# Moving the attention projections next to MLP1 in four groups of a fused transformer block

## The chip, the cores and the metric

The kernel runs on one core of a Trainium2 chip. The metric is the device time of one execution in microseconds (us), the median of several executions; the traces are hardware profiles of one execution each.

## The reference, cut to what matters

```python
x = A_x                                            # 1 x 2048 x 576, bfloat16
h = x + attention(layernorm(x), A_wqkv) @ A_wo     # 32 heads of 18, window of 8 keys, 2 apart
y = layernorm(h)                                   # called LN2 below
h2 = h + gelu(y @ B_w1 + B_b1) @ B_w2 + B_b2       # MLP1: 576 -> 4608; MLP2: 4608 -> 576
```

## The kernel before

The 2048 rows are 16 tiles of 128, worked off in eight groups of two. I number the groups from 1; the code's `k` is one less. A group's stretch on TensorE is MLP1 (`pm` in the profile, 64-row tiles), MLP2 (`po`, 128 rows), and somewhere in it the output projection of the attention (`pw`, 64-row tiles) of the *next* group's two tiles, called c and d. VectorE computes the attention of later groups meanwhile, and LN2 of c and d follows the projection: VectorE adds x (`ln2_h`), ScalarE takes the statistics (`ln2_act`), GpSimd the inverse root, ScalarE writes the normalised tile (`ln2_send`), which is stored to memory and read back transposed (`hnT`) as the input of the next group's MLP1.

In groups 3 to 8 MLP2 is a fast matrix product of the Strassen-Winograd kind: for a part of the rows (`rows`: 12 of 18 blocks in groups 4 and 5, 16 in group 6, all in 7 and 8) seven products instead of eight, and the rest as plain products.

```python
    PRODUCTS = {
        1: (lambda m: h_block(0, 0, m, m + 1), lambda m: w2_block(0, 0, m, m + 1)),
        2: (lambda m: h_block(1, 0, m, m + 1), lambda m: w2_block(1, 0, m, m + 1)),
        3: (lambda m: s_slot(3, m, m + 1), lambda m: w2_block(1, 1, m, m + 1)),
        4: (lambda m: h_block(1, 1, m, m + 1), lambda m: t_slot(3, m, m + 1)),
        5: (lambda m: s_slot(0, m, m + 1), lambda m: t_slot(0, m, m + 1)),
        6: (lambda m: s_slot(1, m, m + 1), lambda m: t_slot(1, m, m + 1)),
        7: (lambda m: s_slot(2, m, m + 1), lambda m: t_slot(2, m, m + 1)),
    }
    # ...
    def product(n, bank, m0, m1):
        lhs, rhs = PRODUCTS[n]
        for m in range(m0, m1):
            mm(bank, lhs(m), rhs(m), n in (1, 7) and m == 0, m == m1 - 1)

    def plain(i, half, bank, rows):
        for m in range(rows, NM):
            for odd in range(2):
                mm(bank, h_block(odd, i, m, m + 1), w2_block(odd, half, m, m + 1), False, m == NM - 1 and odd == 1)
```

The products share PSUM banks. Products 1 and 2 both add to bank `a`; a ScalarE copy "b" carries what product 1 alone made into bank `b`, on which product 6 goes on; "d" carries that to product 5's bank.

```python
    def mlp2_fast(g, rows, tags, wo, hooks):
        p, q, r, s = tags
        last = wo is None
        j0, j1 = g
        af = psum_pair(q, "po")
        a, f = (af[:, n, 0:HALF] for n in range(2))
        b, d = psum_pair(p, "po")[:, 0, 0:HALF], None
        o0, o1 = (late.tile([P, D], BF16, tag="o_sb", name="o_sb", bufs=2) for _ in range(2))
        bank = {1: a, 2: a, 3: f, 4: b, 6: b}
        # ... (sums into the outputs cut)
        def take():
            bank[7], bank[5] = (psum_pair(tag, "po")[:, 0, 0:HALF] for tag in (r, s))

        lo, hi, all_ = (0, SR), (SR, rows), (0, rows)
        seed = {"b": (1, 6), "d": (6, 5), "f": (5, 3)}
        does = {
            "wo": lambda: wo((r, s)), "e": take, "rest": do_rest, "o1": out1,
            "o0": lambda: out0(int(last), 2), "lo": lambda: out0(0, 1),
            "11": lambda: plain(0, 0, a, rows), "12": lambda: plain(0, 1, f, rows),
            "21": lambda: plain(1, 0, b, rows), "22": lambda: plain(1, 1, bank[5], rows),
        }
        if SR < rows < NM:
            steps = [(1, all_), "b", "wo", "h", "e", (2, all_), "11", (6, lo), (7, lo), "6", "7", (6, hi), "d", (7, hi), "rest", "in",
                     (5, all_), "f", "exp", (4, all_), "21", "22", "o1", "4", (3, all_), "12", "o0", "3"]
        elif rows <= SR:
            steps = [(1, all_), "b", "wo", "h", "e", (2, all_), "11", (6, all_), "d", "6", "7", (7, all_), "rest", "in",
                     (5, all_), "f", "exp", (4, all_), "21", "22", "o1", "4", (3, all_), "12", "o0", "3"]
        elif not last:
            steps = [(1, lo), "wo", (1, hi), "b", "h", "e", (7, lo), (6, all_), "d", "6", "7", (2, all_), (7, hi), "rest", "in",
                     (5, all_), "f", (4, all_), "o1", (3, all_), "o0"]
        else:
            steps = ["e", (1, lo), (7, lo), (1, hi), "b", "h", (7, hi), "rest", (6, all_), "d", (2, all_), "lo",
                     (5, all_), "f", (4, all_), "o1", (3, all_), "o0"]
        for step in steps:
            if isinstance(step, tuple):
                product(step[0], bank[step[0]], *step[1])
            elif step in seed:
                nc.scalar.copy(out=bank[seed[step][1]], in_=bank[seed[step][0]])
            else:
                call([does[step]] if step in does else hooks.get(step, ()))
```

`"wo"` is the projection, `"h"`, `"6"`, `"7"`, `"in"` are places for other engines' work, `"e"` takes the two PSUM pairs that the projection wrote. There are four PSUM pairs in all. What stands at those places, cut:

```python
            rows = ROWS[k]
            home = k % 2
            x = {n: [] for n in ("h", "6", "7", "in", "exp", "4", "3")}
            if k < 6:
                if k == 3:
                    m1[0] += [c_(w2_sums, 8, 12)]
                m1[0] += [c_(pv_sum, d), c_(send_o, d), c_(read_o, d)]
                m1[1] = [c_(accumulate_hs, *g)] if k == 2 else []
                m1[1] += [c_(att_qk_one, f, 1, home ^ 1), c_(att_max, (e, f))]
                m1[3] = []
                if k == 2:
                    m1[3] += [c_(w2_sums, 0, 8)]
                early = {2: (), 3: (0,)}.get(k, (0, 2))
                m1[3] += [c_(h_sums, 0, min(rows, SR), early)]
                x["h"] += [c_(h_sums, 0, min(rows, SR), [t for t in range(4) if t not in early])]
                if k == 5:
                    m1[1] += [c_(w2_sums, 12, 14)]
                    x["h"] += [c_(h_sums, SR, rows), c_(w2_sums, 14, 16)]
                x["exp"] += [c_(exps, e, f), c_(att_den, e, f)]
                # ... (attention of later groups, group 7 and 8's sums cut)
            wo = None
            if c is not None:
                if k == 6:
                    x["h"] = [c_(ln2_h, c), c_(ln2_act, c), c_(ln2_h, d)] + x["h"] \
                        + [c_(ln2_more, d), c_(ln2_rstd, d), c_(ln2_send, c), c_(add_b2, c), c_(add_b2, d), c_(ln2_bias, d)]
                    x["6"] += [c_(ln2_hn, d), c_(ln2_out, d)]
                else:
                    x["h"] = [c_(ln2_stats, c, d)] + x["h"]
                    x["6"] += [c_(ln2_send, c)]
                    x["7"] = [c_(ln2_send, d)] + x["7"]
                x["in"] = [c_(ln2_ins, c, d)] + x["in"]
                wo = lambda tags: wo_visit((c, tags[0]), (d, tags[1]))
            mlp1(g, mlp1_plan(p, q, r, s, (r, s, p)), m1, mid)
            mlp2_fast(g, rows, (p, q, r, s), wo, x)
            p, q, r, s = r, s, p, q
```

Everything is scheduled by hand: each engine runs its instructions in the order of this program.

## Time and profile before

| kernel before | |
|---|---|
| median, three runs | 365.71 us (365.44, 365.71, and 375.73) |
| median, all six runs of the comparison | 365.43 us |
| span of the profiled execution | 363.3 us |
| TensorE busy | 98% |

The unit in which I read this kernel is the stretch from the end of one MLP1 to the end of the next, as TensorE runs in every stretch the same matmuls. In the following view of stretches, one line each for groups 4 to 7, the second number is the length, and then come each engine's busy times.

```profile
199.06:235.55 36.49, 36.49 (x496) 30.11 (x492) 34.58 (x40) 24.03 (x59) 4.47 (x4) 1.00 0.38 87
235.55:272.04 36.49, 36.49 (x496) 30.11 (x492) 33.26 (x39) 24.00 (x59) 3.85 (x4) 1.00 0.36 82
272.04:308.48 36.44, 36.15 (x492) 29.72 (x488) 29.05 (x40) 23.88 (x59) 3.21 (x4) 1.00 0.31 67
308.48:344.23 35.75, 35.75 (x490) 29.53 (x486) 12.41 (x26) 18.43 (x49) 1.43 (x2) 1.00 0.11 29
```

The third busy time is VectorE's.

### The profile page before, as it was taken

What the parts mean: (1) busy time and instruction counts of PE and PEld (TensorE: products, weight loads), DVE (VectorE), ACT (ScalarE), POOL (GpSimd) and SP (SyncE); (2) the same over time, 40 slices, a digit from 0 to 9 for tenths busy, and PEclk for the clock granted to TensorE, in tenths of its full rate; (3) what the DMA queues carried; (4) which work ended last, traced back from release to release, by engine and by line L of the source; (5) the groups of instructions that cost most, each with busy time, mean ns of one, the idle gap of its engine ahead of it and who ended that gap; (6) DMA issues with size and microseconds to landing.
All of it is one profiled execution on the core that took longest, in us unless ns stands there. A gap on an engine that the chain in (4) does not pass through costs nothing.

```text
span 363.3 us, 11427 instructions
## 1 busy us (share of the span) xinstructions
PE 357.6 (98%) x4895; PEld 290.5 (80%) x4895; DVE 300.6 (83%) x426; ACT 228.9 (63%) x507; POOL 39.4 (11%) x47
## 2 busy tenths in 40 slices
PE   8999999999999999999999999999999999999996
PEld 4688877888788877887788778877887788778874
DVE  5999999999999999999999899979998498720431
ACT  4779856799526763668556855685568656615630
POOL 2251004000120030103100211020101010100000
PEclk9999999999999999999999999999999999999999
DMA  7989899964445733720552145304530352030001
GB/s 235 299 204 306 223 260 236 363 219 78 145 89 107 218 111 87 152 40 34 137 106 71 35 125 115 72 32 109 118 71 33 74 102 56 3 89 19 2 2 33
DMA packets 61908, 43.70 MB, mean 120 GB/s; under 512 B 31889, under 2 KB 60177, under 8 KB 61857
## 3 DMA queue, kind: packets, MB, share of 16 engines
q1 hardware_dynamic: 59968, 41.13, 41.1%
q0 software_dynamic: 1728, 1.77, 4.8%
q8 instruction: 38, 0.62, 0.7%
q10 hardware_dynamic: 160, 0.07, 0.1%
q14 instruction: 14, 0.11, 0.1%
HBM read 21.10 MB, written 12.42 MB: 92 GB/s over the span
## 4 chain that ended last, share of the span: by engine, by line
PE 94%; DMA 2%; ACT 1%; SPq 1%; DVE 0%; issue 0%
PE pm L217 39%; PE po L667 25%; PE pq L217 14%; PE po L579 10%; PE pw L217 5%; DMA wq_sb<-in_A_wqkv_dram 1%; SPq L104 1%; PE xt_pt L182 1%; DMA x_all<-b_bc 1%; ACT hn L175 0%; ACT hn L479 0%; PE h_pt L182 0%; PE o_pt L182 0%; DVE h L461 0%; ACT hn L478 0%
## 5 line engine op out<-in xcount | busy, mean ns | idle before, releaser
L560 ACT ACTIVATE h_all<-pm,b_sb 128x256 f16<-128x256 f32 (+1 forms) x288 | 108.3, 496 | 74.3 <-PE pm L217 74.3
L217 PE MATMUL pm<-hnT,w_sb 64*128 64x256 bf16 x2304 | 143.0, 269 | 0.0
L217 PEld LDWEIGHTS <-w_sb 64*128 64x128 bf16 x2304 | 111.6, 94 | 15.1 <-issue 1.7
L667 PEld LDWEIGHTS <-h_all 128*128 128x128 f16 x528 | 50.8, 98 | 14.9 <-issue 2.5
L217 PE MATMUL pq<-wq_sb,xnT 64*128 64x288 bf16 x768 | 54.5, 283 | 0.8 <-DMA wq_sb<-in_A_wqkv_dram 0.7
L217 PEld LDWEIGHTS <-xnT 64*128 64x128 bf16 x864 | 42.4, 94 | 11.3 <-issue 1.1
L351 DVE TENSOR_TENSOR prod<-prod 128x2304 bf16<-128x2304 bf16 (+1 forms) x64 | 44.2, 691 | 2.1
L667 PE MATMUL po<-w2a_sb,h_all 128*128 128x288 bf16 (+1 forms) x302 | 42.0, 286 | 0.0
L397 DVE TENSOR_TENSOR prod<-kv_ring,probs 128x4608 bf16<-128x4608 bf16 x16 | 40.9, 2554 | 0.8 <-DMA kv_ring<-kv_dram 0.5
L345 DVE TENSOR_TENSOR prod<-kv_ring,q_all 128x4608 bf16<-128x4608 bf16 x16 | 40.8, 2549 | 0.2
L217 PE MATMUL pm<-hnT,w1h_sb 64*128 64x256 bf16 x288 | 39.2, 269 | 0.0
L403 DVE TENSOR_TENSOR prod<-prod 128x2304 bf16<-128x2304 bf16 (+1 forms) x32 | 33.8, 1057 | 1.0
L579 PEld LDWEIGHTS <-h_all 128*128 128x128 bf16 x288 | 27.8, 98 | 7.9 <-issue 1.0
L481 POOL TENSOR_TENSOR ln_rstd<-ln_var,mhalf 128x1 f32<-128x1 f32 x13 | 14.5, 1115 | 175.1 <-ACT ln_var L480 175.1
L667 PEld LDWEIGHTS <-kv_ring 128*128 128x128 f16 x240 | 23.5, 98 | 6.4 <-issue 0.5
L579 PE MATMUL po<-w2a_sb,h_all 128*128 128x288 bf16 x224 | 28.5, 286 | 0.0
L647 DVE TENSOR_TENSOR kv_ring<-h_all 128x1536 f16<-128x1536 f16 (+3 forms) x10 | 6.9, 687 | 17.3 <-ACT h_all L560 17.3
L667 PE MATMUL po<-w2b_sb,h_all 128*128 128x288 bf16 (+1 forms) x142 | 21.2, 286 | 0.0
L217 PE MATMUL pw<-wo_sb,oT 64*128 64x288 bf16 x256 | 19.5, 283 | 0.0
L162 POOL TENSOR_TENSOR ln_rstd<-ln_veps,mhalf 128x1 f32<-128x1 f32 (+2 forms) x14 | 13.3, 954 | 48.2 <-DVE ln_veps L156 31.8
L217 PEld LDWEIGHTS <-oT 64*128 64x128 bf16 x288 | 13.5, 94 | 4.8 <-issue 1.7
L739 ACT COPY po<-po 128x288 f32<-128x288 f32 x18 | 6.9, 384 | 16.2 <-PE po L667 13.0
(117 smaller groups left out, 383.1 us busy)
## 6 DMA issues: line engine op xcount, KB each, us to landing
w_sb<-in_B_w_dram SPq DMA_DIRECT2D x6, 768.0 KB, 5.5
kv_ring<-kv_dram SPq DMA_DIRECT2D x28, 144.0 KB, 2.6
w2a_sb<-in_B_w_dram SPq DMA_DIRECT2D x4, 1008.0 KB, 6.6
kv_dram<-kv_ring SPq DMA_DIRECT2D x13, 288.0 KB, 3.3
out_dram<-o_sb SPq DMA_DIRECT2D x15, 144.0 KB, 2.5
td<-q_all SPq DMA_DIRECT2D x14, 144.0 KB, 2.2
td<-hn SPq DMA_DIRECT2D x14, 144.0 KB, 1.8
x_all<-in_A_x_dram SPq DMA_DIRECT2D x12, 144.0 KB, 2.9
```

Of the source, the lines that this page charges most:

```text
L162: nc.gpsimd.tensor_tensor(out=rstd[:], in0=veps[:], in1=mhalf[:].to_broadcast([P, n]), op=ALU.pow)
L217: last = nc.tensor.matmul(duo["g"][r ^ swap][i], lhsT=lhsT, rhs=rhs, start=(swap == 0 and i == 0 and kt == 0), stop=(swap == 1 and kt == K ...
L345: nc.vector.tensor_tensor(out=prod[:], in0=k_ring[j % 2], in1=q_all[:, j, :].unsqueeze(1) .to_broadcast([P, W, D]), op=ALU.mult)
L351: nc.vector.tensor_tensor(out=prod[:, :, o * H:o * H + n], in0=prod[:, :, a * H:a * H + n], in1=prod[:, :, c * H:c * H + n], op=ALU.add)
L397: nc.vector.tensor_tensor(out=prod[:].rearrange("p w (d h) -> p w d h", h=H), in0=v_ring[j % 2].rearrange("p w (d h) -> p w d h", h=H), in ...
L403: nc.vector.tensor_tensor(out=prod[:, 0:n, :], in0=prod[:, 0:n, :], in1=prod[:, n:2 * n, :], op=ALU.add)
L481: nc.gpsimd.tensor_tensor(out=rstd[:], in0=var[:], in1=mhalf[:], op=ALU.pow)
L560: pace[0] = nc.scalar.activation(out=hT(grp)[:, f, 0:N], in_=ps[:, r, i * N:(i + 1) * N], func=ACT.Gelu_apprx_tanh, bias=b1_sb[:, f:f + 1] ...
L579: nc.tensor.matmul(banks[half], lhsT=hT(grp)[:, f, i * P:(i + 1) * P], rhs=w2_rows(f)[:, half * HALF:(half + 1) * HALF], start=(f == 0), s ...
L647: nc.vector.tensor_tensor(out=s_slot(t, m0, m1), in0=a, in1=b, op=alu)
L667: nc.tensor.matmul(bank, lhsT=l, rhs=r, start=start, stop=stop, skip_group_check=True)
L739: nc.scalar.copy(out=bank[seed[step][1]], in_=bank[seed[step][0]])
```

## The change

The intent: every change between 64-row and 128-row work costs TensorE a pause, and a projection in the middle of MLP2 costs two of them more than one that stands right behind MLP1, which works on 64 rows too. Groups 4 to 7 put the projection there. As its time no longer lies between product 1 and product 2, product 7 is put there, and the plain rows go between products 6 and 5. Group 3, the QKV part and the last group keep their orders. The core of the diff (cut: names, the tags' order in the callers, and group 7's own places, where the LN2 statistics are split in the same way and VectorE makes the sums of rows 12 to 18 in four instructions instead of eight):

```diff
-        if SR < rows < NM:
-            steps = [(1, all_), "b", "wo", "h", "e", (2, all_), "11", (6, lo), (7, lo), "6", "7", (6, hi), "d", (7, hi), "rest", "in",
-                     (5, all_), "f", "exp", ...
-        elif rows <= SR:
-            steps = [(1, all_), "b", "wo", "h", "e", (2, all_), "11", (6, all_), "d", "6", "7", (7, all_), "rest", "in",
-                     (5, all_), "f", "exp", ...
+        if rows < NM:
+            steps = [(1, all_), "b", "wo", "hc", "h", "e", (2, all_), "11", (6, all_), "d", "6", "7", (7, all_), "rest"] if rows < SR \
+                else ["wo", "hc", (1, all_), "b", "h", "e", (7, lo), (2, all_), (6, all_), "6", "d", "rest", "7", "11"] if rows == SR \
+                else ["wo", (1, all_), "b", "hc", "h", "e", (7, lo), (2, all_), (6, all_), "6", "d", "7", "11", (7, hi), "rest"]
+            steps += ["in", (5, all_), "f", "exp", ...
         elif not last:
-            steps = [(1, lo), "wo", (1, hi), "b", "h", "e", (7, lo), (6, all_), "d", "6", "7", (2, all_), (7, hi), "rest", "in", ...
+            steps = ["wo", "hc", (1, all_), "b", "h", "e", (7, lo), (6, all_), "6", "d", "7", (2, all_), (7, hi), "rest", "in", ...
 ...
-                early = {2: (), 3: (0,)}.get(k, (0, 2))
+                early = () if k == 2 else (0, 2)
 ...
-                    x["h"] = [c_(ln2_stats, c, d)] + x["h"]
+                    x["hc"] = [c_(ln2_h, c), c_(ln2_act, c)] + x["hc"]
+                    x["h"] = [c_(ln2_h, d), c_(ln2_act, d), c_(put_b2, c), c_(put_b2, d)] + x["h"]
                     x["6"] += [c_(ln2_send, c)]
                     x["7"] = [c_(ln2_send, d)] + x["7"]
```

More of the change, by code (lines that the diff above doesn't have):

```diff
@@ L685, in mlp2_fast @@
     def mlp2_fast(g, rows, tags, wo, hooks):
-        p, q, r, s = tags
         last = wo is None
+        q, p, r, s = tags
         j0, j1 = g
@@ L722, in mlp2_fast @@
         }
-        if SR < rows < NM:
-            steps = [(1, all_), "b", "wo", "h", "e", (2, all_), "11", (6, lo), (7, lo), "6", "7", (6, hi), "d", (7, hi), "rest", "in",
-                     (5, all_), "f", "exp", (4, all_), "21", "22", "o1", "4", (3, all_), "12", "o0", "3"]
-        elif rows <= SR:
-            steps = [(1, all_), "b", "wo", "h", "e", (2, all_), "11", (6, all_), "d", "6", "7", (7, all_), "rest", "in",
-                     (5, all_), "f", "exp", (4, all_), "21", "22", "o1", "4", (3, all_), "12", "o0", "3"]
+        if rows < NM:
+            steps = [(1, all_), "b", "wo", "hc", "h", "e", (2, all_), "11", (6, all_), "d", "6", "7", (7, all_), "rest"] if rows < SR \
+                else ["wo", "hc", (1, all_), "b", "h", "e", (7, lo), (2, all_), (6, all_), "6", "d", "rest", "7", "11"] if rows == SR \
+                else ["wo", (1, all_), "b", "hc", "h", "e", (7, lo), (2, all_), (6, all_), "6", "d", "7", "11", (7, hi), "rest"]
+            steps += ["in", (5, all_), "f", "exp", (4, all_), "21", "22", "o1", "4", (3, all_), "12", "o0", "3"]
         elif not last:
-            steps = [(1, lo), "wo", (1, hi), "b", "h", "e", (7, lo), (6, all_), "d", "6", "7", (2, all_), (7, hi), "rest", "in",
+            steps = ["wo", "hc", (1, all_), "b", "h", "e", (7, lo), (6, all_), "6", "d", "7", (2, all_), (7, hi), "rest", "in",
                      (5, all_), "f", (4, all_), "o1", (3, all_), "o0"]
@@ L1015 @@
             home = k % 2
-            x = {n: [] for n in ("h", "6", "7", "in", "exp", "4", "3")}
+            x = {n: [] for n in ("hc", "h", "6", "7", "in", "exp", "4", "3")}
             if k < 6:
@@ L1040 @@
                 m1[3] = [c_(h_sums, 0, SR)]
-                mid[3] = {1: [c_(h_sums, SR, 16)]}
-                x["h"] += [c_(h_sums, 16, NM)]
+                if k == 7:
+                    mid[3] = {1: [c_(h_sums, SR, 16)]}
+                    x["h"] += [c_(h_sums, 16, NM)]
             if k + 3 < len(GROUPS):
@@ L1048 @@
                 if k == 6:
-                    x["h"] = [c_(ln2_h, c), c_(ln2_act, c), c_(ln2_h, d)] + x["h"] \
-                        + [c_(ln2_more, d), c_(ln2_rstd, d), c_(ln2_send, c), c_(add_b2, c), c_(add_b2, d), c_(ln2_bias, d)]
+                    x["hc"] += [c_(ln2_h, c), c_(ln2_act, c)]
+                    x["h"] += [c_(ln2_h, d), c_(ln2_more, d), c_(ln2_rstd, d), c_(h_sums, SR, NM), c_(ln2_send, c),
+                               c_(ln2_bias, d), c_(add_b2, c), c_(add_b2, d)]
                     x["6"] += [c_(ln2_hn, d), c_(ln2_out, d)]
                 else:
-                    x["h"] = [c_(ln2_stats, c, d)] + x["h"]
+                    x["hc"] = [c_(ln2_h, c), c_(ln2_act, c)] + x["hc"]
+                    x["h"] = [c_(ln2_h, d), c_(ln2_act, d), c_(put_b2, c), c_(put_b2, d)] + x["h"]
                     x["6"] += [c_(ln2_send, c)]
@@ L1058 @@
             mlp1(g, mlp1_plan(p, q, r, s, (r, s, p)), m1, mid)
-            mlp2_fast(g, rows, (p, q, r, s), wo, x)
-            p, q, r, s = r, s, p, q
+            if wo and rows >= SR:
+                mlp2_fast(g, rows, (s, p, q, r), wo, x)
+                p, q, r, s = q, r, p, s
+            else:
+                mlp2_fast(g, rows, (q, p, r, s), wo, x)
+                p, q, r, s = r, s, p, q
 _INS = ['A_x', 'A_wqkv', 'A_wo', 'B_x', 'B_w1', 'B_b1', 'B_w2', 'B_b2']
```

## The prediction

> **What bounds the kernel now.** I number the eight groups of two row tiles from 1, as the title of the change does, so the code's k is one less. I read four views, in this order: the page, the chain that ended last, TensorE's waits, and the timelines of the seams in groups 4 to 7. The page first:
>
> ```profile
> PE 357.6 (98%) x4895; PEld 290.5 (80%) x4895; DVE 300.6 (83%) x426; ACT 228.9 (63%) x507; POOL 39.4 (11%) x47
> PE   8999999999999999999999999999999999999996
> PE 94%; DMA 2%; ACT 1%; SPq 1%; DVE 0%; issue 0%
> ```
>
> TensorE is busy for 98% of the span and is 94% of the chain. The kernel is bound by the stream of matmuls, and the change removes no matmul: the counts per engine of the built programs are equal on TensorE and ScalarE, and VectorE has four instructions fewer. So only time *between* matmuls can be won or lost. The waits of TensorE after the start-up are one line:
>
> ```profile
> PE po L667 <- ACT po L739: 0.3, 1, 0.3
> ```
>
> The columns are the total in us, the number of waits and the longest. One wait for one ScalarE copy. The chain of group 5 (code k = 4), beside that of group 2, where the projection already stands next to MLP1:
>
> ```profile
> 124.51 2.21 PE pw L217 x36
> ...
> 217.92 17.79 PE pm L217 x324
> 235.71 1.58 PE po L667 x12
> 237.29 2.31 PE pw L217 x36
> ```
>
> The columns are start, length, work. The same 36 projection matmuls (pw) take 2.21 us behind MLP1 (pm) and 2.31 us behind a product (po). The timeline of the seam in group 5, TensorE's rows:
>
> ```profile
> 235.65 1.65 PE L667 MATMUL po<-w2a_sb,h_all 128*128 128x288 bf16 x12
> 237.22 0.67 PE L217 MATMUL pw<-wo_sb,oT 64*128 64x288 bf16 x8
> ...
> 239.53 2.13 PE L667 MATMUL po<-w2a_sb,h_all 128*128 128x288 bf16 x16
> ...
> 242.49 1.63 PE L667 MATMUL po<-q_all,kv_ring 128*128 128x288 f16 x12
> 243.96 1.63 PE L667 MATMUL po<-w2a_sb,h_all 128*128 128x288 f16 x12
> ```
>
> Twelve matmuls of one product take 243.96 - 242.49 = 1.47 us when the next is of the same kind, and 237.22 - 235.65 = 1.57 us when the projection follows, which works on 64 rows instead of 128. The single starts of the trace say the same: usual steps are 106 ns for a pair of MLP1 and 122 ns for a product; over a change they are 201 to 202 ns and 218 to 219 ns, and the first step after it is 11 ns long. One change of row mode costs 96 + 11 = 107 ns.
>
> **What the skill says.** The Trainium skill, "TensorEngine Tiling (Array Packing)", section "Key Properties": "Mode switching requires drain". The trace agrees, at 107 ns for each switch. "TensorE: Matmul & The Clock Gate", section "Back-to-back issue gap", gives N/2.4 + 2.5 ns, so 122.5 ns for 288 columns; the trace has 122 ns, so there is no slack inside the stream. "Perfetto Trace Analysis", section "Identifying Performance Opportunities", says that a repeating gap on the saturated engine can come from too few buffers for the next tile. Before there is no such gap; below I expect one in group 4, because all four PSUM pairs are in use at the seam.
>
> **The change part by part.**
>
> *Switches.* In groups 4 to 7 before, the order is MLP1 (64 rows), product 1 (128), projections (64), products (128), MLP1: four switches a group. After, it is MLP1, projections, products, MLP1: two. 4 groups x 2 x 0.107 = 0.86 us saved, on the path, as no other engine has to be ready for it.
>
> *The copy in group 6.* This is where the one wait lies:
>
> ```profile
> 282.65 0.41 PE L667 MATMUL po<-w2b_sb,h_all 128*128 128x288 f16 x2
> 283.34 0.53 PE L667 MATMUL po<-x_all,kv_ring 128*128 128x288 f16 x3 [0.29 <-ACT po L739]
> ```
>
> Product 5 starts on a bank that ScalarE seeds with a copy ("d"), and ScalarE does both LN2 sends first. The start of the last matmul before it is 282.77, the step to 283.34 is 571 ns instead of 122: 0.45 us lost (the 0.29 is counted from the modelled end). After, only one send (about 1.1 us) precedes "d". ScalarE by my count, from durations of this stretch: MLP1 ends at 272.04, projections 2.30, product 1 of 16 matmuls to 276.31, its copy to about 276.9, two statistics of 1.9 each to 280.7, one send to 281.9, "d" seen at about 282.35. TensorE by then: product 7 (12), 2 (16), 6 (16), plain rows (4) and the rest of 7 (4) at 0.1224 each, so product 5 is due at 282.68. The wait goes: 0.45 us saved, with 0.3 us to spare.
>
> *Product 7 in second place.* It writes to the PSUM pair of the first projection, so VectorE must have added x to that projection (ln2_h) before. In group 4 VectorE is late:
>
> ```profile
> 200.12 0.69 DVE L365 TENSOR_TENSOR logits<-logits,peak 128x512 f32<-128x512 f32 x1
> 200.73 0.95 DVE L647 TENSOR_TENSOR kv_ring<-h_all 128x1536 f16<-128x1536 f16 x1
> 202.67 1.42 DVE L461 TENSOR_TENSOR h<-pw,x_all 128x576 f32<-128x576 f32 x2 [0.98 <-PE pw L217]
> ```
>
> Without a gap it runs up to 201.7, and then has 0.98 us idle. The change puts a second h_sums piece into that gap (group 4 now makes pieces 0 and 2 before, not 0 alone), about 0.98 us as its likeness in group 5 (235.27 to 236.25). ln2_h then starts at 200.73 + 2 x 0.98 = 202.69, and its reader in group 4 started 0.79 us after it (ScalarE at 203.46), so product 7 may write at about 203.46. TensorE is ready earlier: last pair of MLP1 at 198.96, + 0.11 + 2.30 + 12 x 0.1224 + 0.01 = 202.84. A new wait of 0.62 us. The same sum in group 5: VectorE starts h_sums at 235.27, ln2_h at 237.23, free at 238.0; TensorE needs it at 239.33: none. Group 6: h_sums at 273.24, ln2_h at 275.21, free at 276.0; needed at 276.31: none, by 0.3 us. Group 7: VectorE is only 12.4 of 35.8 us busy there: none.
>
> *Plain rows between 6 and 5, and the rest.* They are the same matmuls elsewhere and cover the copy "d": in groups 4 and 5 twelve of them, 1.47 us. Group 7 makes its sums of rows 12 to 18 in four instructions of 6 blocks instead of eight of 4 and 2; VectorE has room for either. The projections start 1.6 to 2.3 us earlier, so their transposed inputs must have landed: the later one of group 4 lands at 199.41 and is wanted at about 199.67, of group 7 at 308.69 and 309.1; in groups 5 and 6 there is over 2 us. No wait, but two narrow ones.
>
> The sum: - 0.86 - 0.45 + 0.62 = - 0.69 us, so 365.7 becomes 365.0.
>
> **The rivals.** (a) No new wait in group 4: if the second piece costs less or TensorE reaches product 7 later than I count, the gain is the full 1.31 us and the time 364.4. For it: the 0.62 us is the difference of two long sums, each good to about 0.1 us, and of a reader's delay (0.79 us) taken from ScalarE and not from TensorE. Against it: VectorE has no gap from 178.97 to 201.7, and nothing in group 3 moves to make it earlier. (b) Other waits take the place: the projection's transpose in group 4 or 7 (slack 0.3 to 0.4 us, while such transposes land after 2.8 to 4.3 us), or product 7 in group 6 (0.3 us). Each would cost 0.2 to 0.8 us; two of them make it 365.5 to 366, no gain at all. For it: DMA times differ between executions. Against it: of the eight transposes in question seven took 2.8 to 3.0 us, and the slow one (4.3 us) is the one in group 4 that is in time all the same. (c) A wait that repeats in every group, such as for the PSUM pair of product 1, which the last MLP1 evacuation but one must free: that evacuation ends about 1.2 us after MLP1, the product comes 2.3 us after it. Four waits of 1 us would make 368; I see nothing that speaks for it. (d) The switch saving is hidden by something else: not with TensorE at 98% and 94% of the chain.
>
> **Range and chances.** The runs of before at full speed are 365.44 and 365.71, so 0.2 us is noise. Rivals (a) and (b) set the ends: 364.2 to 365.8. Two per cent is 7.3 us, more than five times all that is in the sum; gaining it is out of reach, and losing it would need several waits of the size of a whole product in each group, or mostly slow-state runs, of which before has one (375.73). So faster 0.01, same 0.97, slower 0.02.
>
> **What would show it.** The number of row-mode changes on TensorE falls by eight, and pw takes 2.21 us instead of 2.31 in groups 4 to 7. The wait of TensorE for ScalarE's copy in group 6 is gone. A new wait of TensorE for VectorE's h, 0.5 to 0.7 us, stands ahead of product 7 in group 4 and in no other group. Group lengths, from MLP1's end to the next MLP1's end (36.49, 36.48, 36.44 and 35.75 us before), become 36.9, 36.3, 35.8 and 35.5. The prediction is wrong in its mechanism if the eight changes do not give 0.8 to 0.9 us, in its sizes if group 4 has no wait, and in its scope if a wait for a transposed input (oT) or a second one for VectorE appears.

## The result, and the profile after

| | before | after |
|---|---|---|
| median (runs of the comparison) | 365.43 us (6 runs) | 366.67 us (6 runs, 366.30 to 367.36) |
| ratio | | 1.0037, 95% interval 1.0024 to 1.0051 |
| span of the profiled execution | 363.3 us | 364.8 us |

A ratio is the mean time of one kernel's runs over that of the other's of the same rounds, so not quite the ratio of the medians. Executions over 1.5% slower than the fastest of the same kernel are left out of the means. The change made the kernel 0.4% slower.

The page of after: TensorE's share of the span is as before, but the chain is not.

```profile
PE 358.2 (98%) x4895; PEld 293.0 (80%) x4895; DVE 300.3 (82%) x422; ACT 229.1 (63%) x507; POOL 39.0 (11%) x47
...
PE 65%; DVE 24%; DMA 3%; ACT 3%; issue 2%; SPq 1%; POOL 1%; DVEq 0%; POOLq 0%
```

TensorE falls from 94% of the chain to 65%, and VectorE comes in with 24%. These shares are not lost time, as TensorE is still busy for 98%: from one short wait of TensorE the chain goes back through the engine that it waited for, and through all the work before. So it only says that TensorE now waits for others. Its waits after the start, some of them (the total, the number, the longest; the third line is that of its weight loads):

```profile
PE pm L217 <- DMA hnT<-td: 1.1, 1, 1.1
...
PE po L667 <- ACT po L738: 0.7, 1, 0.7
...
PEld L217 <- DMA oT<-td: 0.6, 2, 0.4
```

The same stretches as before, groups 4 to 7:

```profile
199.32:237.02 37.70, 36.77 (x496) 30.17 (x492) 35.15 (x40) 24.07 (x59) 4.19 (x4) 1.00 0.37 84
237.02:273.29 36.27, 36.27 (x496) 30.28 (x492) 33.08 (x39) 23.95 (x59) 4.28 (x4) 1.00 0.37 83
273.29:310.23 36.94, 35.86 (x493) 31.83 (x489) 28.95 (x40) 23.95 (x59) 3.02 (x4) 1.00 0.28 65
310.23:345.77 35.54, 35.54 (x490) 29.86 (x484) 11.96 (x22) 18.45 (x49) 1.10 (x2) 1.00 0.11 29
```

Groups 5 and 7 are 0.22 and 0.21 us shorter, which is two changes of row mode each. Groups 4 and 6 are 1.21 and 0.50 us longer. The timeline of group 4's seam, some rows (start, length, instruction):

```profile
202.87 1.41 DVE L461 TENSOR_TENSOR h<-pw,x_all 128x576 f32<-128x576 f32 x2
203.65 0.68 ACT L478 ACTIVATE hn<-h 128x576 bf16<-128x576 f32 x1 [1.38 <-DVE h L461]
...
205.56 0.39 ACT L738 COPY po<-po 128x288 f32<-128x288 f32 x1
...
206.00 1.63 PE L667 MATMUL po<-w2a_sb,h_all 128*128 128x288 bf16 x12 [0.70 <-ACT po L738]
```

Product 2 (206.00) waits for the copy "b" (205.56), and the copy stands on ScalarE behind the statistics of tile c, which began at 203.65 because VectorE came late. The single starts of TensorE's matmuls give the losses against the usual step: 0.25 us in the projection (its transposed input of d landed late), 0.30 us ahead of product 7 (VectorE's `ln2_h`), 0.87 us ahead of product 2. Group 6:

```profile
285.05 0.43 SPq L194 DMA_DIRECT2D td<-hn  x1
...
288.26 2.53 SPq L496 DMA_TRANSPOSE hnT<-td  x2
...
292.53 0.61 PE L217 MATMUL pm<-hnT,w_sb 64*128 64x256 bf16 x8 [1.08 <-DMA hnT<-td]
```

The same store and reads in the kernel before:

```profile
283.39 0.43 SPq L194 DMA_DIRECT2D td<-hn  x1
285.01 3.21 SPq L496 DMA_TRANSPOSE hnT<-td  x2
```

The last small store of tile d is issued at 285.05, the transposing reads wait for it until 288.26, 3.21 us after its issue instead of 1.62 before, and group 7's MLP1 waits for them: 1.15 us by the starts.

The account: eight changes of row mode at 0.107 us, - 0.86; the copy "d" of group 6, - 0.45; new waits 0.25 + 0.30 + 0.87 in group 4 and 1.15 in group 6, + 2.57. Sum + 1.26 us; the four stretches are together 146.45 - 145.17 = 1.28 us longer. The spans differ by 1.5 us, as this execution also came out of the start-up 0.26 us later (end of the first MLP1 at 87.05 against 86.79 us), which the change does not touch.

### The profile page after: what moved, and what is told of

The parts are those of the page before. It is cut to its first block, busy times and chain, and to the rows that moved or that the text cites. A ratio compares the mean times of both kernels' runs of the same rounds, so it can differ in the third digit from the quotient of the medians.

```text
span 364.8 us, 11419 instructions
## 1 busy us (share of the span) xinstructions
PE 358.2 (98%) x4895; PEld 293.0 (80%) x4895; DVE 300.3 (82%) x422; ACT 229.1 (63%) x507; POOL 39.0 (11%) x47
## 4 chain that ended last, share of the span: by engine, by line
PE 65%; DVE 24%; DMA 3%; ACT 3%; issue 2%; SPq 1%; POOL 1%; DVEq 0%; POOLq 0%
PE pm L217 24%; PE po L667 20%; PE pq L217 14%; DVE prod L351 4%; DVE prod L397 4%; DVE prod L345 4%; PE pw L217 3%; DVE prod L403 3%; PE po L579 1%; DMA wq_sb<-in_A_wqkv_dram 1%; DMA kv_ring<-kv_dram 1%; DVE h L461 1%; SPq L104 1%; DVE den L391 1%; DMA hnT<-td 1%
## 5 line engine op out<-in xcount | busy, mean ns | idle before, releaser
L217 PEld LDWEIGHTS <-w_sb 64*128 64x128 bf16 x2304 | 113.5, 94 | 14.5 <-issue 2.8
L647 DVE TENSOR_TENSOR kv_ring<-h_all 128x1536 f16<-128x1536 f16 (+4 forms) x9 | 6.7, 745 | 17.2 <-ACT h_all L560 17.2
```

The lines of the kernel that those rows point to most:

```text
L217: last = nc.tensor.matmul(duo["g"][r ^ swap][i], lhsT=lhsT, rhs=rhs, start=(swap == 0 and i == 0 and kt == 0), stop=(swap == 1 and kt == K ...
L647: nc.vector.tensor_tensor(out=s_slot(t, m0, m1), in0=a, in1=b, op=alu)
```

## The experiments

Nine kernels ran, one of them twice (e8 and e12), all with correct results. Kernels of one call shared the runs of the kernel before, whose medians were 365.25, 365.17 and 365.30 us. What tells most is the length of the four stretches in each one's trace, read from the starts of TensorE's matmuls:

| kernel | group 4 | group 5 | group 6 | group 7 | median us | ratio (95%) |
|---|---|---|---|---|---|---|
| before | 36.49 | 36.49 | 36.44 | 35.75 | 365.43 | |
| after | 37.70 | 36.27 | 36.94 | 35.54 | 366.67 | 1.0037 (1.0024 to 1.0051) |
| e1 copy first | 36.88 | 37.28 | 36.75 | 35.54 | 366.72 | 1.0037 (1.0022 to 1.0052) |
| e2 packets shifted | 37.43 | 36.27 | 36.47 | 35.54 | 367.47 | 1.0063 (1.0045 to 1.0081) |
| e3 sends first | 37.80 | 36.27 | 36.37 | 35.54 | 365.84 | 1.0012 (0.9997 to 1.0027) |
| e4 group 4 old | 36.48 | 36.27 | 37.42 | 35.54 | 366.54 | 1.0043 (1.0008 to 1.0078) |
| e5 only 5 and 7 | 36.49 | 36.27 | 36.44 | 35.54 | 364.92 | 0.9998 (0.9980 to 1.0015) |
| e7 second before seventh | 36.97 | 36.27 | 36.82 | 35.54 | 366.67 | 1.0055 (1.0023 to 1.0086) |
| e8 group 4 old, 6 mended | 36.49 | 37.71 | 35.78 | 35.54 | 364.62 | 0.9984 (0.9969 to 0.9999) |
| e10 packets shifted again | 37.69 | 36.27 | 35.78 | 35.54 | 366.69 | 1.0043 (1.0026 to 1.0061) |
| e11 only 6 (mended) and 7 | 36.48 | 36.49 | 35.78 | 35.54 | 364.32 | 0.9966 (0.9935 to 0.9998) |
| e12 = e8 again | 36.48 | 36.27 | 35.78 | 35.54 | 364.15 | 0.9958 (0.9924 to 0.9992) |

Apart from these stretches the traces differ almost only in the start-up: the first MLP1 ends between 86.7 and 88.2 us (latest in e7; at 89.5 in e2, which has a longer warm-up). So one execution can be 1.5 us longer than another although its groups are not, and a median need not follow the sum of its row.

My theories: **A**, product 2 waits in group 4 because the copy "b" reads the bank that product 2 adds to, and stands behind statistics on ScalarE; its rival **B**, VectorE's lateness is what product 2 waits for. **C**, group 7's MLP1 waits because one of TensorE's 16 KB instruction packets meets the last small store of tile d on one of the 16 DMA engines; its rival **D**, because ScalarE now sends tile d behind the copy "d".

**e1: the copy ahead of the statistics, in groups 4 and 5.**

```diff
-  ["wo", "hc", (1, all_), "b", "h", "e", (7, lo), (2, all_), ...]   # rows == 12
+  ["wo", (1, all_), "b", "hc", "h", "e", (7, lo), (2, all_), ...]
```

> The changed kernel with one edit: in groups 4 and 5 ScalarE makes the copy of product 1's bank ahead of the LN2 statistics of the first tile instead of behind them (as group 6 has it already). Theory A (the second product waits because it adds to the bank that this copy reads, and the copy stands behind 1.9 us of statistics on ScalarE): TensorE's 0.87 us wait ahead of product 2 in group 4 falls below 0.15 us, the other two waits of that group (0.25 for the transposed input, 0.30 ahead of product 7) and the 1.15 us at the start of group 7's MLP1 stay, and the time falls by 0.7 to 0.9 us, from 366.7 to about 365.9. Rival B (product 2 waits for VectorE, whose sums come late in group 4, and the copy only happened to end at the same time): the wait stays above 0.5 us and the time stays within 0.3 us of 366.7.

In group 4 the wait ahead of product 2 is gone, as A has it: one wait is left, 0.61 us ahead of product 7. But the time did not fall (366.72 us, the figure of B, so that here only the trace parts the two), because group 5 got a wait of 1.01 us that I had not expected:

```profile
242.03 2.55 DVE L345 TENSOR_TENSOR prod<-kv_ring,q_all 128x4608 bf16<-128x4608 bf16 x1
...
242.38 4.00 POOL L481 TENSOR_TENSOR ln_rstd<-ln_var,mhalf 128x1 f32<-128x1 f32 x2 [23.43 <-ACT ln_var L480]
...
245.04 0.29 ACT L486 ACTIVATE ln_nmean<-ln_nmean,ln_rstd 128x1 f32<-128x1 f32 x1 [0.92 <-POOL ln_rstd L481]
...
246.58 0.65 PE L667 MATMUL po<-x_all,kv_ring 128*128 128x288 f16 x4 [0.85 <-ACT po L738]
```

With the copy first, the statistics of tile c start 1.56 us later after MLP1's end than in the changed kernel. GpSimd's inverse root, one number per row, which took 0.63 us there, now begins within VectorE's long multiply (242.03 to 244.58); it and the next one took 4.0 us together. ScalarE's send waits 0.92 us for it, the copy "d" stands behind the send, and product 5 behind the copy. The Trainium skill, "SBUF — State Buffer", section "SBUF: two separate sides", says that a VectorE instruction with two SBUF inputs and a GpSimd instruction that reads SBUF take a shared port in turn, for the whole instruction. The traces here agree: in all twelve of them the 60 inverse roots that began within this multiply ended 0.41 to 0.42 us after it and so took 0.75 to 2.86 us, and the 12 that began within a VectorE reduction, which has one input, took 0.56 us.

**e2: TensorE's instruction packets shifted.** The profile's queue 8 is named "instruction" and carries 38 packets in the kernel before, one for about 256 of TensorE's 9790 instructions. The warm-up at the start, where TensorE waits for its first loads, got more matmuls, so that every later packet comes earlier.

```diff
-        for n in [512] * 8 + [P] * 5:
+        for n in [512] * 5 + [64] * 43 + [P] * 5:
```

> The changed kernel with 40 more tiny matmuls in the warm-up, where TensorE waits for the first loads anyway (three of its 512-column matmuls give way to 43 of 64 columns). Nothing else moves, but TensorE's 16 KB instruction packets, one for about 256 of its instructions, come 40 products (4.9 us) or 40 MLP1 matmuls (2.2 us) earlier. Theory C (the 1.15 us wait of group 7's MLP1 comes of one such packet, 1.05 us long, that meets the last small store of the normalised tile on one of the DMA engines, so that the store lands after 3.1 us instead of 1.6): the store in group 6 lands within 2 us, the wait falls below 0.3 us and the time falls by 0.8 to 1.2 us, to about 365.6. Rival D (the wait comes of ScalarE's order, which sends the second tile behind the copy for product 5): the wait stays above 0.8 us and the time at 366.7. The waits in group 4 should stay in both cases, but for that of the transposed input, which another packet may hit or miss.

In group 6 the store landed after 1.56 us and group 7's MLP1 did not wait, although the store was issued later after MLP1's end (12.4 us) than in the changed kernel (11.8 us). That speaks for C. The time missed the expectation by 2 us: the warm-up was too long and the start-up ended 2.5 us later (first MLP1 ends at 89.50 us). Group 6 also had a new wait, 0.69 us ahead of product 7, as VectorE was late there in this execution, and group 4's MLP1 waited 0.27 us for its input.

**e3: both sends ahead of the copy "d", in group 6.**

```diff
-                    x["6"] += [c_(ln2_send, c)]
-                    x["7"] = [c_(ln2_send, d)] + x["7"]
+                    x["6"] += [c_(ln2_send, c)] + ([c_(ln2_send, d)] if k == 5 else [])
+                    x["7"] = ([] if k == 5 else [c_(ln2_send, d)]) + x["7"]
```

> The changed kernel with one edit: in group 6 ScalarE sends both normalised tiles ahead of the copy for product 5, as the kernel before does. Theory D (ScalarE's order): the second tile goes out about 0.4 us earlier, the wait at group 7's MLP1 falls from 1.15 to 0.5 or less, and product 5 waits for the copy again, by 0.5 to 0.8 us; in sum 366.2 to 366.7. Theory C (the packet): what counts is whether the last small store is still in flight when the packet comes; as it is 0.4 us earlier of 1.3, most likely it is still hit and the wait stays at about 1 us, so the time becomes 367.2 to 367.5, worse than the changed kernel.

MLP1 of group 7 does not wait, and product 5 waits 0.59 us for the copy, as D had it. I had thought the packet would still hit; it came at 286.26, after the store had landed (285.89). So this run does not part C from D: an earlier store avoids both. The time, 365.84 us, is below the figures of both theories.

**e4: group 4 as before.** (The diff restores the old order, tags and early sums for that group.)

> The changed kernel with group 4 as in the kernel before (order of products, PSUM tags, and VectorE's early sums); groups 5 to 7 keep the change. Accounting theory: the three waits of group 4 (0.25 + 0.30 + 0.87 = 1.42 us) go, two changes of row mode come back (0.21 us), so the time falls by 1.2 us to about 365.5, equal to the kernel before within 0.2 us, and the wait of 1.15 us at group 7 stays. Rival (waits move on: DVE or the DMA is late in group 4 in any order, and group 5 takes the wait over): less than 0.6 us comes back.

Group 4 is 36.48 us again, to 0.01 as before, and group 5 has no wait, so its losses were of its own order. But the median fell by only 0.13 us, not the 1.2 expected; by the time alone the rival would be right. The times are in two bunches, 365.37 and 365.51 against 367.56 and 367.94 us. The profiled execution is one of the quick ones and has a wait of 1.63 us at group 7's MLP1. What the other bunch has on top I cannot say, as it was not traced.

**e5: only the two groups without new waits.**

```diff
+        NEW = (4, 6)        # k of the groups that take the new order
```

> Only groups 5 and 7 take the new order, the two in which the trace of the changed kernel shows no new wait; groups 4 and 6 stand as in the kernel before. Accounting theory: four changes of row mode fewer, 0.43 us; group 5 takes 36.27 us instead of 36.49, group 7 35.54 instead of 35.75, group 6 keeps its 0.45 us wait for the copy, and the time is 364.9 against 365.3 of the kernel before. Rival (the freed time is taken by a wait elsewhere, a transfer that a TensorE instruction packet meets): some group is longer by 0.4 us or more and the times are equal.

The trace has what the sum says, - 0.22 and - 0.21 us, and no new wait. Five of six runs lie at 364.72 to 365.38 and one at 366.82 us, so the ratio is no proof of 0.1%. The median is 0.25 us lower than that of the kernel before, where 0.43 was due.

**e7: in group 4 the copy first and product 2 ahead of product 7.**

```diff
+                else ["wo", (1, all_), "b", "hc", "h", "e", (2, all_), (7, lo), (6, all_), "6", "d", "rest", "7", "11"]   # group 4 alone
```

> The changed kernel with two edits in group 4 alone: ScalarE's copy of product 1's bank ahead of the LN2 statistics, and product 2 ahead of product 7. Theory A: product 2 then waits for the copy alone, which is seen 0.44 us after product 1 ends, and product 7 finds VectorE done; group 4 takes 36.27 + 0.44 = 36.7 us (37.7 in the changed kernel, 36.9 with the copy first and product 7 second, 36.5 before). The wait at group 7's MLP1 stays at about 1.1 us, so the time is about 365.7. Rival B (VectorE is what group 4 waits for in any order): 36.9 or more.

Group 4 took 36.97 us, with a single wait, 0.68 us ahead of product 2 (I had said 0.44). The rows show the term that was too small:

```profile
204.54 0.38 ACT L739 COPY po<-po 128x288 f32<-128x288 f32 x1 [1.10 <-issue]
...
204.97 1.75 PE L667 MATMUL po<-w2a_sb,h_all 128*128 128x288 bf16 x13 [0.52 <-ACT po L739]
```

The last matmul of product 1 started at 204.17, its successor could have started at 204.29, and the copy itself starts only 0.25 us after that. So a copy between two products on one bank costs 0.68 us when nothing stands between them, more than the 0.21 us that the changed place of the projection saves in a group. By its figure for the length (36.9 or more) this run is B's. But product 7 does not wait here, and the one wait is for the copy, which no longer stands behind VectorE's work; so B's reason does not hold, and A's copy was under-counted. The time, 366.67 us, missed the expected 365.7 by 1.0 us: in the profiled execution the start-up was 1.4 us longer than in the kernel before, which the edit does not touch.

**e10: the packets shifted again, with a shorter warm-up.**

```diff
-        for n in [512] * 8 + [P] * 5:
+        for n in [512] * 2 + [64] * 40 + [P] * 5:
```

> The changed kernel with 34 more matmuls in the warm-up, now with as much time in the warm-up as before (two of 512 columns, 40 of 64), so that the start should not be later as it was with 40 more. Theory C (the instruction packet): in group 6 it comes about 4 us earlier, the last small store of the normalised tile lands in 1.5 to 2 us, and the wait at group 7's MLP1, 1.15 us in the changed kernel, is below 0.3 us, though ScalarE's order is that of the changed kernel. Theory D (order alone): the wait stays at 0.8 us or more. A second packet may meet another transfer instead (a projection's input); if so, the trace names it. Time by theory C, if none does: 365.6.

Group 6 took 35.78 us, without any wait, in the changed kernel's own order of instructions on all engines:

```profile
285.79 0.43 SPq L194 DMA_DIRECT2D td<-hn  x1
...
287.41 2.53 SPq L496 DMA_TRANSPOSE hnT<-td  x2
...
292.05 0.61 PE L217 MATMUL pm<-hnT,w_sb 64*128 64x256 bf16 x8
```

The store and the reads stand 1.62 us apart here and 3.21 us in the changed kernel. For nine of the twelve traces (times in us; landings from the semaphores, packets from the transfer records; in the other three, e5, e11 and e12, the store took 1.5 us, the packet came after it had landed, and nothing waited):

| kernel | small store of d issued | landed | packet starts | MLP1 of group 7 waits |
|---|---|---|---|---|
| after | 285.05 | 288.18 | 285.96 | 1.15 |
| e1 | 284.94 | 287.97 | 285.94 | 0.96 |
| e4 | 283.48 | 286.94 | 284.48 | 1.63 |
| e7 | 285.56 | 288.50 | 286.45 | 0.96 |
| before | 283.39 | 284.94 | 285.45 | 0 |
| e2 | 288.19 | 289.75 | 284.27 | 0 |
| e3 | 284.35 | 285.89 | 286.26 | 0 |
| e8 | 283.07 | 284.62 | 286.90 | 0 |
| e10 | 285.79 | 287.33 | 283.96 | 0 |

Where a packet starts about 1 us after the store is issued, the store takes 2.9 to 3.5 us and MLP1 waits; in the other rows it takes 1.5 to 1.6 us and MLP1 does not. In the changed kernel 8 of the store's 128 packets start only at 287.0 to 287.1, when the 1.05 us packet is over; the rest of them started by 286.2. Eight of 128 is the share of one DMA engine of 16, if they share evenly; which engine a packet used is not in the trace. In e10 itself the packet (283.96) comes upon the small store of tile c, issued at 284.18: that one took 2.20 us, and nothing waited for it. The Trainium skill, "Runtime: NRT & Kernel Launch", section "Instruction fetch mechanics", says that instructions come in blocks of 16 KiB, 256 instructions, and that this is mostly hidden; the size and the spacing agree here, and what is not hidden is the delay of a neighbour. The time of e10 did not fall (366.69 us): it left the start-up 0.7 us later than the changed kernel, and its runs go from 366.12 to 368.12 us, more widely than I can account for with one trace.

**e8 and e12: group 4 as before, group 6 with three edits.** In group 6 VectorE adds x to the first projection between its first two pieces of sums, ScalarE takes its statistics ahead of the copy "b", and both tiles are sent ahead of "d":

```diff
-                else ["wo", (1, all_), "b", "hc", "h", "e", (7, lo), ...]          # rows == 16
+                else ["wo", "hc", (1, all_), "b", "h", "e", (7, lo), ...]
-                early = () if k == 2 else (0, 2)
+                early = () if k == 2 else (0,) if k in (3, 5) else (0, 2)
+                # k == 5: h_sums piece 2 behind ln2_h(c), ln2_act(c) in "hc"; ln2_send(d) in "6"
```

> Group 4 as in the kernel before, groups 5 and 7 as in the changed kernel, and group 6 in the new order with three edits: VectorE adds x to the first projection right behind its first piece of sums, ScalarE takes the LN2 statistics of it ahead of the copy of product 1's bank, and both normalised tiles go out ahead of the copy for product 5. Theory A + D (orders on ScalarE and VectorE): ScalarE saves 1.9 us ahead of the sends, so that neither product 5 nor group 7's MLP1 waits; groups 4 to 7 take 36.5, 36.3, 35.8 and 35.5 us, 1.1 us less than before in sum, and the time is 364.2. If the order on ScalarE is not what made the waits, a wait of 0.4 us or more stays in group 6 and the time is 364.9 or more.

Group 6 took 35.78 us, as expected, without a wait (which of the three edits it needs was not tested); the median is 364.62 us where 364.2 was expected. Group 5, unchanged since the changed kernel, took 37.71 us in the profiled execution, the slowest of the six:

```profile
224.20 2.56 DVE L397 TENSOR_TENSOR prod<-kv_ring,probs 128x4608 bf16<-128x4608 bf16 x1 [2.02 <-DMA kv_ring<-kv_dram]
...
239.26 1.41 DVE L461 TENSOR_TENSOR h<-pw,x_all 128x576 f32<-128x576 f32 x2
```

A load of v rows landed after 5.1 us (2.5 in the trace of e4), VectorE stood still for 2.0 us, reached `ln2_h` that much later, and TensorE waited 0.58 us ahead of product 7 and 0.87 ahead of product 2: the same two waits as in group 4 of the changed kernel, now in group 5, because VectorE was late for another reason. To see if that was one execution, the same kernel ran again.

> The kernel with group 4 as before and group 6 with three edits once more, for a second trace of it. In its first trace VectorE waited 2.0 us in group 5 for a load of v rows that landed after 5.1 us, and TensorE then waited 1.4 us at the seam. If that is a matter of one execution, this trace shows group 5 at 36.3 us and a span of about 362.4, and most runs lie at 363.7 to 364.7; if it is of the order of instructions, group 5 takes 37 us or more again and the median is 364.6 or more.

The second trace has 36.48, 36.27, 35.78 and 35.54 us, all as expected, and six runs at 363.99 to 364.58 us. From its chain:

```profile
236.31 2.21 PE pw L217 x36
238.52 16.27 PE po L667 x132
254.79 17.79 PE pm L217 x324
272.58 2.20 PE pw L217 x36
274.79 15.79 PE po L667 x128
```

TensorE passes from piece to piece without a break. The span was 362.8 us, not the 362.4 that I expected, as the start-up was 0.6 us slower than that of the kernel before (first MLP1 ends at 87.39).

**e11: groups 6 (mended) and 7 alone.**

```diff
+        NEW = (5, 6)
```

> Groups 4 and 5, whose seam VectorE reaches late, as in the kernel before; group 6 in the new order with its three edits, group 7 in the new order. Accounting theory: groups 4 to 7 take 36.5, 36.5, 35.8 and 35.5 us, so the time is 0.9 us below the kernel before, 364.3 against 365.2, and the executions spread no more than those of the kernel before (0.75 us), as group 5 no longer has a seam that a late load for VectorE turns into a wait of TensorE. If the spread of the runs with the new order came from something else (the start, group 7), they spread by 1.5 us or more as with group 5 changed.

As expected, no wait in the trace and 364.32 us. The spread is 0.9 us (364.13 to 365.04), a little over the 0.75 foreseen, and that of e12, with group 5 changed, is 0.6: so the spread does not show group 5's seam as the cause, and e12 and e11 cannot be told apart by their times. Their intervals are wide because one run of the kernel before took 369.09 us; without it those runs go from 364.85 to 365.98, and all twelve runs of e11 and e12 but one lie below them.

## Why the prediction was wrong

**Right.** Each change of row mode cost what the prediction took: groups 5 and 7 became 0.22 and 0.21 us shorter in every kernel that has the new order and no wait there, and pw fell from 2.31 to 2.21 us. The wait for the copy "d" in group 6 went, and came back as 0.59 us when e3 put both sends ahead of it again. The wait ahead of product 7 in group 4, predicted as 0.62 us, is 0.30 in the changed kernel, where a late transposed input had already taken 0.25, and 0.61 in e1, where none had.

**Wrong: a term was missing in group 4.** The step that failed is "*Product 7 in second place*", which counts for that group "A new wait of 0.62 us" and nothing further. It followed PSUM for the bank of product 7 and did not ask what product 2 needs. Product 2 adds to the bank that the copy "b" reads, and that copy stands behind the statistics of tile c on ScalarE, which begin only when VectorE has finished `ln2_h`. So VectorE's lateness counts twice: 0.30 us ahead of product 7 and 0.87 ahead of product 2. Before, the projection stood between products 1 and 2, with the copy ahead of the statistics. e1 took the second wait away by the order on ScalarE alone. The prediction did work out the copy for group 6, where it stands first, but never as something that product 2 waits for.

**Wrong: the input of the next MLP1 was left out.** The part on "Plain rows between 6 and 5, and the rest" asked which transposed inputs of the projection would land in time and did not ask it of the other transposed tile, `hnT`, which the sends produce; and "*The copy in group 6*" booked 0.45 us for moving the copy "d" ahead of the second send without asking who waits for that send. In the kernel before it landed at 289.87 with MLP1 due at 290.78. In the changed kernel three things use that up: TensorE reaches the next MLP1 0.66 us sooner, ScalarE sends tile d 0.4 us later after MLP1's end, and the store lands 1.6 us later because of an instruction packet, of which 0.9 us remain at `hnT`, as the reads themselves were quicker (4.1 us from their start to the landing against 4.9). e10 shows that the third is needed for the wait; e3 shows that an earlier send avoids it too.

**Half right: rival (b).** It named the transposed input in group 4, and that wait was there in the profiled execution (0.25 us), but not in e1, e2, e3, e7 or e10, which have the same projection there; so it was chance in part. The prediction had named such a wait as the sign that its scope was wrong. Its range also ended at 365.8 us, though rival (b) by its own sum went to 366, and "more than five times all that is in the sum" holds for the gains (1.31 us), not for all three terms (1.93).

The sum: predicted - 0.86 - 0.45 + 0.62 = - 0.69 us; measured in the traces - 0.86 - 0.45 + 0.30 + 0.25 + 0.87 + 1.15 = + 1.26 us.

**Open.** Why some executions of the kernels with the new order in group 4 or 5 are 1.5 to 4 us longer than others (e4, e5, e7, e10) was seen only once in a trace, in e8, as a late load for VectorE. That the others are of this kind is not shown. A rival is the start-up, which took up to 1.5 us more in some traces with the same warm-up; and the two longest, 369.84 us (e7) and 369.09 (the kernel before), have granted clocks of 0.994 and 0.995, where every other run of the experiments has 0.998 to 1.0, so the order of work need not be the reason.

## What to carry to other kernels

When an order of work on the bound engine is tightened, list for every instruction that moves up all that it waits for, and above all the readers of the bank that it adds to, not only the writer of its inputs; a copy out of a bank that the next product extends cost 0.68 us here if nothing stands between. The freed time must then be looked for at the next seam, where an input that landed 0.9 us early before can land late. A seam may be tightened where the helping engine has room (groups 6 and 7 here) and left alone where it is nearly full (group 4, VectorE busy for 34.6 of 36.5 us).

## What the Trainium skill lacked or had wrong

- "TensorEngine Tiling (Array Packing)" says that a switch of the tiling mode drains TensorE and gives no figure. Here each change between 64-row and 128-row tiles cost 0.107 us, in both directions (steps of 201 and 218 ns instead of 106 and 122, and 11 ns more on the first step after it).
- "Runtime: NRT & Kernel Launch" calls the instruction fetch mostly hidden and has nothing on its effect on other transfers. Here TensorE's 16 KB packets took 0.9 to 1.8 us each on a DMA engine, and a small store that met one landed after 2.9 to 3.5 us instead of 1.5 to 1.6.
- No page has the cost of a ScalarE copy between two accumulations on one PSUM bank. Here TensorE lost 0.68 us: 0.25 until the copy began, 0.38 for the copy, and about 0.05 until the next matmul.
- "SBUF — State Buffer" describes the port that VectorE and GpSimd share, without a figure for such a tiny instruction. Here a GpSimd inverse root of 128 x 1 that began within VectorE's multiply of 2.55 us ended 0.41 to 0.42 us after it (60 in twelve traces, 0.75 to 2.86 us long), against 0.56 us in all when it began within a reduction (12). In e1 two of them took 4.0 us together.
